# Turning q on VectorE and multiplying it in 32x64 tiles of the PE array

## The chip, the core and the metric

The kernel runs on one core of a Trainium2 chip. The metric is the device time of one execution in microseconds (us), the median of several runs. Five engines run side by side, each with its own stream of instructions, and wait for one another only through semaphores: TensorE (PE in the profile; its weight loads are a row of their own, PEld), VectorE (DVE), ScalarE (ACT), GpSimd (POOL) and SyncE (SP), which here starts most DMA transfers. TensorE writes its results to PSUM, which has eight banks of 512 fp32 values for each of 128 partitions. VectorE and ScalarE bring them from there to SBUF.

## What is computed

The program is an attention without softmax followed by a gated feed-forward block. All data are fp32.

```python
batch, n_heads, seq, head_dim = (8, 8, 576, 64)
n_tokens, d_model, d_ff = (4608, 512, 1536)

kv  = np.einsum('bhsd,bhse->bhde', k, v)              # 64 x 64 per head
out = np.einsum('bhsd,bhde->bhse', q, kv)
rms = np.sqrt(np.mean(out * out, axis=-1, keepdims=True) + 1e-06)
x   = (out / rms * g_norm)                            # then (B,H,S,D) -> (B*S, H*D)

gate = 1.0 / (1.0 + np.exp(-(x @ w_gate)))
val  = x @ w_val
return (gate * val @ w_out).astype(np.float32)
```

## The kernel before

The 4608 tokens are handled in nine chunks of 512 (`G`), so a chunk is a little less than one batch of 576. The first chunk and the attention of the first two batches are woven together by hand. From chunk 1 on, both dense layers use a Strassen-like scheme with 7 instead of 8 products (`first_layer_fast`, `second_layer_fast`); their lines are L578 and L664 of the profile. Attention works on pairs of heads: `n` is a pair, four of them (`NHP`) make a batch.

The attention of batch c+1 is put into the gaps of chunk c. It is cut into pieces, which wait in a queue `fill`. After each pair of products of the first dense layer, `slot()` takes one piece from the queue. A block of that layer has seven such slots, p1, p6, p2, p7, p5, p4 and p3, and a chunk has six blocks, so 42 slots.

```python
def slot():
    if fill:
        fill.popleft()()
...
for f in range(NF2):
    one, two = block(f), block(f + NF2)
    for i, (p, r) in enumerate(zip(one[0], two[0])):   # p1, p6, p2, p7, p5, p4, p3
        p()
        r()
        slot()
        ...                                            # sums of weights on GpSimd
    one[1]()                                           # VectorE: h = h * sg, 128x512
    two[1]()
    h_sums(c, f)                                       # VectorE: four sums of 128x256
```

These are the pieces of attention for one pair, as they were (marks of cuts are `...`):

```python
def q_mm():                         # L251: q turned by TensorE, six transposes of 96x128
    d["q"] = ps = at_ps("q")
    for j in range(NJ):
        c0 = NP * (j % JH)
        nc.tensor.transpose(ps[:, j // JH, c0:c0 + NP], pairs[n]["q"][:, j].rearrange("p e d -> p (e d)"),
                            ident[0:NP, 0:NP])

def q_out():                        # L256: copied to SBUF by ScalarE
    d["qT"] = sb.tile([P, 2, JH * NP], FP32, tag="qT", name="qT")
    nc.scalar.copy(out=d["qT"], in_=d["q"][:, :, 0:JH * NP])
    ...

def u_mm():                         # L271: q (k^T v) in tiles of 64 rows x 64 columns
    ps = at_ps("u")
    d["u"] = ps[:, :, 0:NU * HD]
    qT = d["qT"].rearrange("p i n -> p (i n)")
    for i in range(2 * NU):
        t0 = min(PH * i, S - PH)
        r = PH * (i % 2)
        for e in range(2):
            es = slice(HD * e, HD * e + HD)
            nc.tensor.matmul(d["u"][r:r + PH, e, HD * (i // 2):HD * (i // 2) + HD], qT[es, t0:t0 + PH], kv[es],
                             start=True, stop=True)
# then: u_square (ScalarE, 128x640), u_sum (VectorE), u_root (ScalarE), u_norm (VectorE),
# x_mm (L298: five transposes of 128x128 by TensorE), x_out (ScalarE, into xT, times g_norm)
```

The products k^T v of a batch are made at once, in 128x64 tiles (`kv_mm`, L332, and L338 for the rest of 64 tokens), and copied to SBUF by VectorE. The order in the queue was this:

```python
for n in range(NHP * b, NHP * b + NHP, 2):
    ...
    fill.extend([one[Q], one[Q_OUT], two_[Q], two_[Q_OUT]])
    if n == NHP * b:
        fill.extend([idle] * (0 if early else 3) + [kv_mm, kv_out])
    fill.extend([u_of_both, one[U_SQUARE], two_[U_SQUARE], one[U_SUM], two_[U_SUM], one[U_ROOT], one[U_NORM],
                 two_[U_ROOT], two_[U_NORM], one[X], one[X_OUT], two_[X], two_[X_OUT]])
```

In PSUM, attention has two tiles of two banks each, used in turn (`at_ps`), and the dense layers have four single banks (`mm_ps`).

Of the kernel before, what the change touches and what calls it, by code (L numbers as in the profile page):

```python
# [20 lines left out]
def kernel(  # L21
# [16 lines left out]
    P = 128  # L38
# [2 lines left out]
    NP = S // NJ  # L41
    JH = NJ // 2

    PH = P // 2
    NU = -(-S // P)
    UX = P * 3

    NK4 = S // P
    S4 = P * NK4
# [31 lines left out]
    def load_q(n):  # L81
        if n >= B * NHP:
            return
        b, h0 = n // NHP, 2 * (n % NHP)
        pool, bufs = (first, 4) if n < NE else (sb, 2)
        t = pool.tile([NP, NJ, 2, HD], FP32, tag="q", name="q", bufs=bufs)
        for e in range(2):
            nc.sync.dma_start(out=t[:, :, e, :], in_=q[b, h0 + e].rearrange("(p j) d -> p j d", j=NJ))  # L88
        pairs[n]["q"] = t

    kv_late = {}
# [118 lines left out]
    eps = const.tile([P, 1], FP32, name="eps")  # L210
    g_col = const.tile([P, 1], FP32, name="g_col")

    kvs = [const.tile([P, 2, HD], FP32, name=f"kv{i}") for i in range(2)]
    for e in range(2):
        nc.scalar.dma_start(out=g_col[HD * e:HD * e + HD], in_=g_norm.rearrange("(d o) -> d o", o=1))
    make_identity(nc, ident)
# [12 lines left out]
    def attention(n, at_ps):  # L229

        b, m = divmod(n, NHP)
        d = {}
        kv = kvs[n // 2 % 2][:, n % 2]

        def kv_mm():
            d["kv"] = ps = at_ps("kv")
            for j in range(NJ):
                js = slice(HD * j, HD * j + HD)
                for e in range(2):
                    nc.tensor.matmul(ps[HD * e:HD * e + HD, 0, 0:HD], pairs[n]["k"][:, e, js], pairs[n]["v"][:, e, js],  # L240
                                     start=(j == 0), stop=(j == NJ - 1))

        def kv_out():
            nc.vector.tensor_copy(out=kv, in_=d["kv"][:, 0, 0:HD])
            load_kv(n + 4)

        def q_mm():
# [4 lines that stand above are left out]
                                    ident[0:NP, 0:NP])  # L252

        def q_out():
            d["qT"] = sb.tile([P, 2, JH * NP], FP32, tag="qT", name="qT")
            nc.scalar.copy(out=d["qT"], in_=d["q"][:, :, 0:JH * NP])  # L256
            for i in (n + 4,) if n + 4 < NE else (n + 2,) if n + 2 >= NE else ():
                load_q(i)

        def u_mm():  # L260


            ps = at_ps("u")
            d["u"] = ps[:, :, 0:NU * HD]
            qT = d["qT"].rearrange("p i n -> p (i n)")
            for i in range(2 * NU):
                t0 = min(PH * i, S - PH)
                r = PH * (i % 2)
                for e in range(2):
                    es = slice(HD * e, HD * e + HD)  # L270
                    nc.tensor.matmul(d["u"][r:r + PH, e, HD * (i // 2):HD * (i // 2) + HD], qT[es, t0:t0 + PH], kv[es],  # L271
                                     start=True, stop=True)

        def u_square():
            d["sq"] = sb.tile([P, 2, NU * HD], FP32, tag="sq", name="sq")
            nc.scalar.activation(out=d["sq"], in_=d["u"], func=AF.Square)

        def u_sum():
            d["ms"] = sb.tile([P, 2, NU], FP32, tag="ms", name="ms")
            nc.vector.tensor_reduce(out=d["ms"].rearrange("p e i -> p (e i)"),  # L280
                                    in_=d["sq"].rearrange("p e (i d) -> p (e i) d", d=HD), axis=AX.X, op=ALU.add)

        def u_root():
            nc.scalar.activation(out=d["ms"], in_=d["ms"], func=AF.Sqrt, bias=eps, scale=1.0 / HD)

        def u_norm():

            nc.vector.reciprocal(d["ms"], d["ms"])
            d["xn"] = d["sq"].rearrange("p e c -> p (e c)")
            nc.vector.tensor_tensor(out=d["xn"].rearrange("p (i e d) -> p e i d", e=2, d=HD),  # L290
                                    in0=d["u"].rearrange("p e (i d) -> p e i d", d=HD),
                                    in1=d["ms"].unsqueeze(3).to_broadcast([P, 2, NU, HD]), op=ALU.mult)

        def x_mm():
            d["x"] = ps = at_ps("x")
            for i in range(NU):
                bank, c0 = divmod(P * i, UX)
                nc.tensor.transpose(ps[:, bank, c0:c0 + P], d["xn"][:, P * i:P * i + P], ident)  # L298

        def x_out():  # L300

            s0 = 0
            while s0 < S:
                c, o = divmod(S * b + s0, G)
                i, r = divmod(s0, UX)
                n_ = min(G - o, (UX if i == 0 else S - UX) - r)
                nc.scalar.activation(out=chunk(c)[:, m, o:o + n_], in_=d["x"][:, i, r:r + n_], func=AF.Copy, scale=g_col)
                s0 += n_

        return [kv_mm, kv_out, q_mm, q_out, u_mm, u_square, u_sum, u_root, u_norm, x_mm, x_out]  # L310


# [6 lines left out]
    def feed(b):  # L319
# [3 lines left out]

        def kv_mm():
            mains, rest = kv_late[b]
            tiles = [at_ps("kv") for _ in range(2)]
            d["kv"] = tiles
            for n in range(NHP):
                for j in range(NK4):
                    for e in range(2):  # L330
                        c = slice(NK4 * HD * e + HD * j, NK4 * HD * e + HD * j + HD)
                        nc.tensor.matmul(tiles[n // 2][HD * e:HD * e + HD, n % 2, 0:HD], mains[n, "k"][:, c],  # L332
                                         mains[n, "v"][:, c], start=(j == 0), stop=False)
            for i in range(NHP // 2):
                for r in range(2):
                    for e in range(2):
                        n, rs, c = NHP // 2 * r + i, slice(PH * r, PH * r + PH), HD * (2 * i + e)
                        nc.tensor.matmul(tiles[n // 2][HD * e:HD * e + HD, n % 2, 0:HD], rest[rs, c:c + HD],  # L338
                                         rest[rs, GH + c:GH + c + HD], start=False, stop=True)

        def kv_out():
            for kv, ps in zip(kvs, d["kv"]):
                nc.vector.tensor_copy(out=kv, in_=ps[:, :, 0:HD])

        def idle():
            pass

        for n in range(NHP * b, NHP * b + NHP, 2):
            one, two_ = (attention(n + i, at_ps) for i in range(2))

            def u_of_both(one=one, two_=two_):
                one[U]()
                two_[U]()

            fill.extend([one[Q], one[Q_OUT], two_[Q], two_[Q_OUT]])
            if n == NHP * b:
                fill.extend([idle] * (0 if early else 3) + [kv_mm, kv_out])
            fill.extend([u_of_both, one[U_SQUARE], two_[U_SQUARE], one[U_SUM], two_[U_SUM], one[U_ROOT], one[U_NORM],
                         two_[U_ROOT], two_[U_NORM], one[X], one[X_OUT], two_[X], two_[X_OUT]])

    def flush():
        while fill:
# [11 lines left out]
    def store(c, t, ot, cols=slice(0, DM), queues=(nc.sync,)):  # L374

        r0 = i = 0
        while r0 < P:
            b, s = divmod(G * c + P * t + r0, S)
            j, p = divmod(s, NP)
            n = min(P - r0, NP - p)  # L380
            dst = out[S * b:S * b + S, :].rearrange("(p j) d -> j p d", j=NJ)[j, p:p + n, cols]
            queues[i % len(queues)].dma_start(out=dst, in_=ot[r0:r0 + n, cols])
            r0 += n
            i += 1

    psum_at = ctx.enter_context(tc.tile_pool(name="psum_at", bufs=1, space=bass.MemoryType.PSUM))
    psum_ctx = tc.tile_pool(name="psum0", bufs=1, space=bass.MemoryType.PSUM)
    psum0 = psum_ctx.__enter__()  # L390

    def at0_ps():
        return psum_at.tile([P, 2, 512], FP32, tag="at", name="at")

    turns = count()

    def at_ps(kind):
        if next(turns) % 2 == 0:
            return at0_ps()
        return psum.tile([P, 2, 512], FP32, tag="at1", name="at1")  # L400

    def early(n):

# [8 lines left out]
                return t[:, :, JH * P:]  # L412
            return t
        return ps

    def mm_ps():
        return psum.tile([P, 512], FP32, tag="mm", name="mm", bufs=4)


    class Plain:  # L420
# [46 lines left out]
        b3.1.2 b3.0.3 b3.1.3 c4.4  # L467
    """
    blks, copies = {}, {}
    two0 = at0_ps()  # L470
    for token in order.split():
        name = token.rstrip("0123456789.")
        n = [int(i) for i in token[len(name):].split(".")]
# [1 line left out]
        if name == "b":  # L475
            if f not in blks:
# [2 lines left out]
                    psum = ctx.enter_context(tc.tile_pool(name="psum", bufs=1, space=bass.MemoryType.PSUM))  # L479
                    ps = (mm_ps(), mm_ps())  # L480
                else:
                    t = at0_ps() if f else two0
                    ps = (t[:, 0], t[:, 1])
                blks[f] = Plain(0, f, ps)
            blks[f].mm(n[1], n[2])
        elif name == "CG":
# [16 lines left out]
            load_unit(f)  # L503
        elif name == "warm":
            for _ in range(f):
                nc.tensor.matmul(two0[:, 0, 0:P], ident, ident, start=True, stop=True)
        else:
            a[f][steps[name]]()
            if token == f"Q{NE - 1}":
# [1 line left out]
                hp = ctx.enter_context(tc.tile_pool(name="hp", bufs=21))  # L511
    late.extend([blks[3].gate, blks[3].end])
    for f in range(4, NFT):
        plain(0, f, (mm_ps(), mm_ps()))
        if f == NFT - 2:
            load_late(2)

    two1 = [at_ps(None) for _ in range(2)]
    ps = [two1[t % 2][:, t // 2] for t in range(G // P)]

    def second(t, f):
        nc.tensor.matmul(ps[t], gv[0, f][:, P * t:P * t + P], w["wo", f], start=(f == 0), stop=(f == NFT - 1),  # L522
# [256 lines left out]
```

## Time and profile before

| | |
|---|---|
| time, median of 3 runs | 1097.55 us (1096.55 to 1098.04) |
| span of the profiled execution | 1095.0 us |
| TensorE clock granted | 1.00 |
| PE busy | 1088.9 us (99%) |
| DVE busy | 564.4 us (52%) |
| ACT busy | 315.7 us (29%) |
| POOL busy | 278.8 us (25%) |
| DMA moved | 57.73 MB, mean 53 GB/s |

The page of the profile gives busy times for the whole span, the chain of work that ended last, and the costliest groups of instructions. A group's line has the source line, the engine, the operation, the tile that it writes and the tiles that it reads, the shapes and the count, then the busy time in us and the mean of one in ns, and after a second bar the idle time of the engine just before, with what ended it. A matmul of fp32 leaves two records of its own and two of weight loads in the trace; a transpose leaves one of each. An answer by stretches of time gives, for each stretch, its length and what each engine was busy in it. An answer in order of time gives start and length in us, and merges instructions of one kind that follow one another.

### The profile page before, as it was taken

Reading aid. Unit: us, or ns where it says so; the run is one execution under the profiler, and the core shown is the slowest. Engines: PE = TensorE matmul, PEld = TensorE weight load, DVE = VectorE, ACT = ScalarE, POOL = GpSimd, SP = SyncE. Lnnn points to the kernel's source line nnn. Section 1 sums busy time; section 2 is a strip of 40 time slices with the busy share of each in tenths; the row PEclk is TensorE's granted clock in tenths of the full one; section 3 lists DMA queues with packets and bytes.
Section 4 is the critical chain, followed back from the end, with each engine's and each line's share of the span. In section 5 each row is a group of like instructions: output and inputs, shape, how many; then the busy total and the mean of one; then the engine's idle time right before and its main releaser. Section 6 shows DMA issues by size and latency. Waiting matters only on the chain.

```text
span 1095.0 us, 17063 instructions
## 1 busy us (share of the span) xinstructions
PE 1088.9 (99%) x6722; PEld 902.2 (82%) x6722; DVE 564.4 (52%) x1117; ACT 315.7 (29%) x611; POOL 278.8 (25%) x390
## 2 busy tenths in 40 slices
PE   9999999999999999999999999999999999999998
PEld 8544458888888888888888888888888888888888
DVE  4887845762366416561466236641656155615641
ACT  4754322421245114430254014511443011101110
POOL 0000024440244203330344024420333044404410
PEclk9999999999999999999999999999999999999999
DMA  9944711000400040101300040104000100010001
GB/s 246 265 156 154 240 39 23 10 14 20 128 1 22 15 124 11 23 1 50 98 22 1 20 128 1 23 13 119 18 1 1 30 10 1 1 38 2 1 1 39
DMA packets 81519, 57.73 MB, mean 53 GB/s; under 512 B 47392, under 2 KB 75424, under 8 KB 81440
## 3 DMA queue, kind: packets, MB, share of 16 engines
q1 hardware_dynamic: 81184, 56.61, 19.2%
q8 instruction: 54, 0.88, 0.3%
q14 instruction: 25, 0.20, 0.1%
q10 hardware_dynamic: 256, 0.03, 0.0%
HBM read 47.19 MB, written 9.44 MB: 52 GB/s over the span
## 4 chain that ended last, share of the span: by engine, by line
PE 97%; DMA 1%; SPq 1%; DVE 1%; issue 0%; ACT 0%; DVEq 0%
PE mm L578 53%; PE mm L664 26%; PE mm L427 6%; PE at L522 4%; PE at L427 2%; PE at L271 1%; PE at L298 1%; PE at L332 1%; PE at L251 1%; DMA v<-in_v_dram 1%; PE two L240 0%; PE two L271 0%; PE two L298 0%; PE two L251 0%; SPq L78 0%; SPq L88 0%
## 5 line engine op out<-in xcount | busy, mean ns | idle before, releaser
L565 POOL TENSOR_TENSOR tw<-gv 128x256 f32<-128x256 f32 x192 | 138.5, 732 | 765.9 <-PE mm L578 614.3
L578 PE MATMUL mm<-xT,tw 128*128 128x256 f32 x768 | 182.2, 380 | 0.2 <-DVE gv L592 0.2
L578 PE MATMUL mm<-sx,tw 128*128 128x256 f32 x768 | 182.3, 380 | 0.0
L578 PE MATMUL mm<-xT,gv 128*128 128x256 f32 x768 | 181.8, 380 | 0.0
L578 PEld LDWEIGHTS mm<-xT,gv 128*128 128x128 f32 x768 | 144.8, 190 | 19.7 <-issue 0.5
L578 PEld LDWEIGHTS mm<-xT,tw 128*128 128x128 f32 x768 | 144.1, 190 | 19.6 <-issue 0.6
L578 PEld LDWEIGHTS mm<-sx,tw 128*128 128x128 f32 x768 | 144.2, 190 | 19.0
L565 POOL TENSOR_TENSOR tw<-gv,tw 128x256 f32<-128x256 f32 x192 | 145.7, 780 | 0.0
L610 ACT ACTIVATE sg<-sg 128x256 f32<-128x256 f32 x96 | 40.0, 417 | 190.2 <-DVE sg L609 190.2
L600 DVE TENSOR_TENSOR gv<-mm,sg 128x256 f32<-128x256 f32 x96 | 40.8, 425 | 103.1 <-PE mm L578 103.1
L578 PE MATMUL mm<-sx,gv 128*128 128x256 f32 x384 | 91.3, 381 | 0.0
L664 PE MATMUL mm<-w,gv 128*128 128x256 f32 x384 | 88.5, 379 | 0.4 <-DVE gv L617 0.4
L664 PE MATMUL mm<-w,s 128*128 128x256 f32 (+1 forms) x408 | 88.3, 367 | 0.0
L664 PE MATMUL mm<-t2w,gv 128*128 128x256 f32 x384 | 88.1, 379 | 0.0
L586 ACT COPY sg<-mm 128x256 f32<-128x256 f32 x96 | 35.7, 372 | 165.9 <-PE mm L578 162.1
L617 DVE TENSOR_TENSOR gv<-gv,sg 128x512 f32<-128x512 f32 x96 | 82.6, 899 | 0.0
L664 PEld LDWEIGHTS mm<-w,s 128*128 128x128 f32 x408 | 74.1, 190 | 9.4
L664 PEld LDWEIGHTS mm<-w,gv 128*128 128x128 f32 x384 | 72.8, 190 | 10.6 <-DVE gv L617 0.8
L664 PEld LDWEIGHTS mm<-t2w,gv 128*128 128x128 f32 x384 | 72.9, 190 | 9.9
L578 PEld LDWEIGHTS mm<-sx,gv 128*128 128x128 f32 x384 | 72.5, 190 | 10.0
L596 ACT ACTIVATE sg<-mm 128x256 f32<-128x256 f32 x96 | 36.1, 383 | 106.3 <-PE mm L578 106.2
L614 DVE TENSOR_TENSOR gv<-mm,gv 128x256 f32<-128x256 f32 x96 | 40.7, 424 | 48.1 <-PE mm L578 48.1
(97 smaller groups left out, 1092.4 us busy)
## 6 DMA issues: line engine op xcount, KB each, us to landing
q<-in_q_dram SPq DMA_DIRECT2D x64, 144.0 KB, 3.1
st<-in_moe_w_gate_dram SPq DMA_DIRECT2D x12, 512.0 KB, 4.2
st<-in_moe_w_val_dram SPq DMA_DIRECT2D x12, 512.0 KB, 5.1
st<-in_moe_w_out_dram SPq DMA_DIRECT2D x12, 512.0 KB, 4.3
kv<-in_k_dram SPq DMA_DIRECT2D x24, 256.0 KB, 4.8
kv<-in_v_dram SPq DMA_DIRECT2D x24, 256.0 KB, 5.5
out_dram<-sg SPq DMA_DIRECT2D x23, 192.0 KB, 2.3
out_dram<-sg SPq DMA_DIRECT2D x24, 128.0 KB, 2.4
```

Of the source, the lines that this page charges most:

```text
L251: nc.tensor.transpose(ps[:, j // JH, c0:c0 + NP], pairs[n]["q"][:, j].rearrange("p e d -> p (e d)"), ident[0:NP, 0:NP])
L427: nc.tensor.matmul(self.ps[i], w[("wg", "wv")[i], self.f][:, m, :], xT[self.c][:, m, :], start=(m == 0), stop=(m == NMT - 1), skip_group_c ...
L522: nc.tensor.matmul(ps[t], gv[0, f][:, P * t:P * t + P], w["wo", f], start=(f == 0), stop=(f == NFT - 1), skip_group_check=True)
L565: nc.gpsimd.tensor_tensor(out=tw[f, i], in0=b[in0], in1=b[in1] if isinstance(in1, tuple) else tw[f, in1], op=ALU.subtract)
L578: nc.tensor.matmul(ps, wt[:, m, :], xs[:, m, :], start=(new and m == 0), stop=(m == NK - 1), skip_group_check=True)
L586: nc.scalar.copy(out=d["sg"][:, h2], in_=pa)
L596: nc.scalar.activation(out=d["sg"][:, h1], in_=d["pa"], func=AF.Sigmoid)
L600: tt(out=d["h"][:, h2], in0=d["pb"], in1=d["sg"][:, h2], op=ALU.add)
L610: nc.scalar.activation(out=d["sg"][:, h2], in_=d["sg"][:, h2], func=AF.Sigmoid)
L614: tt(out=d["h"][:, h1], in0=d["pc"], in1=d["h"][:, h1], op=ALU.add)
L617: tt(out=d["h"], in0=d["h"], in1=d["sg"], op=ALU.mult)
L664: nc.tensor.matmul(ps, hs(f), ws[:, f, :], start=(new and f == 0), stop=(f == NF2 - 1), skip_group_check=True)
```

## The change

Turning q leaves TensorE. VectorE transposes it in blocks of 32x32, which puts the 64 head dimensions of a head not on 64 partitions but on 32 partitions twice, for three row blocks of 32 tokens (`NQ = 3`) side by side. The contraction over 64 is therefore made in two steps of 32 (`NC = 2`), accumulated in PSUM, and it runs in tiles of 32 rows and 64 columns of the array: three row blocks by two column halves. Each row block needs k^T v on its own 32 partitions, so VectorE copies it there (`kv_copies`). The order of tokens within a batch changes with this, and the stores follow it.

Two pairs now go through the steps together, nine slots from their products to the transposes of x. That needs four PSUM banks in one piece for attention, in place of twice two; the dense layers still take four banks in turn, now from two pools of two. The tiles for turned q, for k^T v and for the squares are allocated once (`qTs`, `kvs`, `kvq`, `sqs`). The aim is to take work from TensorE.

```diff
@@ load_q
+        else:
+            t = sb.tile([NP, 2, NJ * HD], FP32, tag="q", name="q")
+            nc.sync.dma_start(out=t, in_=q[b, h0:h0 + 2].rearrange("h (p j) d -> p h (j d)", j=NJ))
@@ constants
-    kvs = [const.tile([P, 2, HD], FP32, name=f"kv{i}") for i in range(2)]
+    kvs = const.tile([P, NHP, HD], FP32, name="kvs")
+    kvq = const.tile([NP, NHP, 2 * NC, HD], FP32, name="kvq")
+    qTs = const.tile([P, 2, 2 * NJ * HD], FP32, name="qTs")
+    sqs = const.tile([P, 2 * NU * P], FP32, name="sqs")
@@ feed(b)
+        def kv_out():
+            nc.vector.tensor_copy(out=kvs, in_=d["kv"][:, :, 0:HD])
+
+        def kv_copies(i):
+            for r in range(NQ):
+                nc.vector.tensor_copy(out=kvq[QB * r:QB * r + QB, :, i], in_=kvs[QB * i:QB * i + QB])
+
+        def turn(n):
+            for e in range(2):
+                w_ = NJ * HD
+                nc.vector.transpose(qTs[0:NP, n % 2, w_ * e:w_ * e + w_],
+                                    pairs[n]["q"][:, e].rearrange("p (j i c) -> p i j c", i=NC, c=QB))
+            load_q(n + 2)
+
+        def two_pairs(n0):
...
+            def u_mm():
+                d["u"] = u = at_ps()[:, 0:NQ, 0:2 * QC]
+                for s in range(3):
+                    for e in range(2):
+                        for i in range(NC):
+                            for r in range(NQ):
+                                for half in range(2):
+                                    which, g = divmod(2 * s + half, 3)
+                                    c = NJ * HD * e + QC * i + PH * g
+                                    nc.tensor.matmul(u[PH * half:PH * half + PH, r, P * s + HD * e:P * s + HD * e + HD],
+                                                     qTs[QB * r:QB * r + QB, (n0 + which) % 2, c:c + PH],
+                                                     kvq[QB * r:QB * r + QB, (n0 + which) % NHP, NC * e + i],
+                                                     start=(i == 0), stop=(i == NC - 1))
...
+            def u_sum(i):            # half of the heads in a slot, and u_norm likewise
+                nc.vector.tensor_reduce(out=ms[:, :, units[i]], in_=by_head(sq)[:, :, units[i]], axis=AX.X, op=ALU.add)
...
+            def x_mm():
+                d["x"] = x = at_ps()
+                for r in range(NQ):
+                    for s in range(3):
+                        nc.tensor.transpose(x[:, r, P * s:P * s + P], sq[:, r, P * s:P * s + P], ident)
...
+            return [u_mm, u_square, lambda: u_sum(0), lambda: u_sum(1), u_root, lambda: u_norm(0), lambda: u_norm(1),
+                    idle, x_mm, lambda: x_out(0), lambda: x_out(1)]
@@ the queue
-        (the loop shown above)
+        n0 = NHP * b
+        fill.extend([lambda: turn(n0), lambda: turn(n0 + 1)] + [idle] * (0 if early else 5) + [kv_mm, kv_out])
+        fill.extend([lambda i=i: kv_copies(i) for i in range(2 * NC)])
+        fill.extend(two_pairs(n0))
+        fill.extend([lambda: turn(n0 + 2), lambda: turn(n0 + 3)])
+        fill.extend(two_pairs(n0 + 2))
@@ store: rows of batches from 2 on
+                r, c0 = divmod(s, QC)
+                n = min(P - r0, QC - c0)
+                queues[i % len(queues)].dma_start(
+                    out=rows.rearrange("(r p j) d -> r j p d", p=QB, j=NJ)[r, c0 // QB:(c0 + n) // QB],
+                    in_=ot[r0:r0 + n, cols])
@@ PSUM
+    def mm_ps():
+        if next(turns) % 4 < 2:
+            return psum.tile([P, 512], FP32, tag="mm", name="mm", bufs=2)
+        return mm0_ps()
+
+    def at_ps():
+        return psum.tile([P, 4, 512], FP32, tag="at", name="at")
@@ the end of chunk 0
-        plain(0, f, (mm_ps(), mm_ps()))
+        if f == NFT - 1:
+            last = at_ps()
+            plain(0, f, (last[:, 0], last[:, 1]))
+        else:
+            plain(0, f, (mm_ps(), mm_ps()))
...
-    two1 = [at_ps(None) for _ in range(2)]
-    ps = [two1[t % 2][:, t // 2] for t in range(G // P)]
+    ps = [mm_ps() for _ in range(G // P)]
```

## The prediction

> **What bounds the kernel now.** I read the engines' busy shares and the chain that ended last first, then busy time by stage, then the order in time of the weight loads around each piece of attention, and last the groups of VectorE. The page says that TensorE is the bound from end to end:
>
> ```profile
> PE 1088.9 (99%) x6722; PEld 902.2 (82%) x6722; DVE 564.4 (52%) x1117; ACT 315.7 (29%) x611; POOL 278.8 (25%) x390
> ...
> PE 97%; DMA 1%; SPq 1%; DVE 1%; issue 0%; ACT 0%; DVEq 0%
> ```
>
> A busy TensorE need not be a full one, so the reader should see what one chunk costs with and without attention. Below are two stretches (start:end, length, then busy time and instructions of PE, PEld, DVE, ACT, POOL). The first is a chunk of 512 tokens whose gaps hold the attention of one batch; the second is a chunk after the last batch, with the same two dense layers and nothing between.
>
> ```profile
> 636.40:755.10 118.70, 118.70 (x789) 104.18 (x789) 56.97 (x124) 35.83 (x72) 34.26 (x48) 1.00 0.15 40
> ...
> 873.80:982.60 108.80, 108.80 (x506) 95.78 (x505) 52.33 (x110) 15.55 (x40) 36.06 (x48) 1.00 0.04 10
> ```
>
> So one batch of attention adds 118.70 - 108.80 = 9.90 us, six times over (batches 2 to 7). The first two batches run in a hand-ordered start that the change leaves alone. What the change can win or lose is in these 6 x 9.9 = 59 us.
>
> Next the order in time of the weight loads. Without anything between them, one slot of dense work (8 loads) starts 1.73 us after the one before. In turn: a turn of q (L251), the products of two pairs (L271), five transposes of x (L298), the k^T v of a batch (L332, L338).
>
> ```profile
> 402.95 1.70 PEld L578 LDWEIGHTS mm<-xT,gv 128*128 128x128 f32 x8
> 404.68 0.69 PEld L251 LDWEIGHTS at<-ident,q 96*128 96x128 f32 x6
> 405.31 1.60 PEld L578 LDWEIGHTS mm<-xT,tw 128*128 128x128 f32 x8
> 406.93 1.70 PEld L578 LDWEIGHTS mm<-sx,tw 128*128 128x128 f32 x8
> ```
>
> ```profile
> 332.47 1.70 PEld L578 LDWEIGHTS mm<-xT,tw 128*128 128x128 f32 x8
> ...
> 334.50 1.26 PEld L271 LDWEIGHTS at<-kv,qT 64*64 64x64 f32 x80 [0.33 <-issue]
> ...
> 335.82 1.59 PEld L578 LDWEIGHTS mm<-sx,gv 128*128 128x128 f32 x8
> ...
> 337.44 1.70 PEld L578 LDWEIGHTS mm<-xT,gv 128*128 128x128 f32 x8
> ```
>
> ```profile
> 351.26 0.69 PEld L298 LDWEIGHTS at<-ident,sq 128*128 128x128 f32 x5
> 351.91 1.60 PEld L578 LDWEIGHTS mm<-sx,tw 128*128 128x128 f32 x8
> 353.53 1.70 PEld L578 LDWEIGHTS mm<-xT,gv 128*128 128x128 f32 x8
> ```
>
> ```profile
> 412.11 1.70 PEld L578 LDWEIGHTS mm<-xT,gv 128*128 128x128 f32 x8
> 414.14 1.95 PEld L332 LDWEIGHTS at<-kv 128*64 128x64 f32 x64 [0.33 <-issue]
> 416.16 0.32 PEld L338 LDWEIGHTS at<-kv 64*64 64x64 f32 x16
> 416.55 1.59 PEld L578 LDWEIGHTS mm<-sx,tw 128*128 128x128 f32 x8
> ```
>
> From the starts: a turn of q costs 405.31 - 404.68 = 0.63, and the slot behind it is 1.62 instead of 1.73, so 0.52 us net. Two pairs of products cost 0.30 of waiting before (334.50 - 332.47 = 2.03 instead of 1.73), 1.32 themselves, less 0.11: 1.51. Five transposes of x: 0.65 - 0.11 = 0.54. The k^T v: 0.30 + 2.41 - 0.11 = 2.60. Per batch 4 x 0.52 + 2 x 1.51 + 4 x 0.54 + 2.60 = 9.86, which is the 9.90 above: TensorE loses nothing to waits in these chunks, and what is taken from it counts in full.
>
> The tiles matter. In the products four tiles of 64x64 work side by side. Their 80 load records span 1.26 us less one load of 0.135, so 1.125 us for 20 rounds of four, 0.057 us a round. The k^T v has two tiles of 128x64: 64 records in 1.95 - 0.14 = 1.81 us are 32 rounds of two, also 0.057 us. A round of 64 columns costs the same whether two or four tiles share it, so the tile is the limit there and not the rate of issue.
>
> **What the Trainium skill says.** "TensorEngine Tiling (Array Packing)", section "Tiling Modes", gives eight tiles for 32x64, which load and multiply independently, and says that changing the mode drains the array; the constant round and the 0.30 us before L271 agree with both, for 64x64. Its section "Restrictions and Gotchas" wants different row tiles in different PSUM banks; the new code has row block r in bank r. "TensorE: Matmul & The Clock Gate", section "Wait — 56ns, not 53.3ns?", gives a floor of about 25 ns between starts of small matmuls. The trace has 80 records in 1.40 us, 17.5 ns each, below that; but these are 40 matmuls of the program, two records each, so 29 ns per matmul stay above it, and a floor per program matmul is not excluded. "VectorE: DVE Perf Modes", section "The three transpose paths", says that VectorE transposes within 32x32 blocks only and needs 311 ns for 128x128 of bf16; no run here shows it yet.
>
> **The change, part by part, per batch.**
> Turning q on TensorE goes: 4 x 0.52 = -2.08 us, with ScalarE's four copies of 0.64 us, off the path. VectorE now does it in 8 transposes of 96x384. Of the skill's 311 ns, 133 would be 128 elements at its 0.96 GHz, leaving 0.18; with 384 elements (0.40 us) that makes an estimate of 0.58 us each, 4.6 us in all.
> The products of two pairs become 72 program matmuls, 144 records, on six tiles (three row blocks by two column halves) instead of 80 records on four. If six tiles share a round as four did, that is 24 rounds of 0.057 = 1.37 us against 20 rounds = 1.14, so +0.23 for two pairs and +0.46 per batch. The entry and exit around it (1.51 - 1.14 = 0.37) stay.
> Turning x: nine transposes for two pairs in place of ten, at 0.54 / 5 = 0.108: -0.11 for two pairs, -0.22 per batch. Two pieces in place of four save little, as 0.54 is already five full transposes.
> The k^T v stays at 2.60. Behind it come 12 new copies of 32x256 on VectorE, which spread it over the row blocks.
> Sum on TensorE: -2.08 + 0.46 - 0.22 = -1.84 us per batch, six times -11.0 us.
>
> What VectorE gives back as waits. Its groups (line, engine, shapes, count, busy us, mean ns, idle before):
>
> ```profile
> L617 DVE TENSOR_TENSOR gv<-gv,sg 128x512 f32<-128x512 f32 x96 | 82.6, 899 | 0.0
> ...
> L592 DVE TENSOR_TENSOR gv<-mm,sg 128x256 f32<-128x256 f32 x96 | 38.3, 420 | 45.9 <-PE mm L578 45.2
> ...
> L280 DVE TENSOR_REDUCE ms<-sq 128x10 f32<-128x640 f32 x32 | 25.5, 810 | 4.5 <-ACT sq L276 4.5
> ...
> L343 DVE COPY kv<-at 128x128 f32<-128x128 f32 x12 | 2.9, 281 | 0.0
> ```
>
> A copy of 128 elements takes 281 ns, so I take 0.3 to 0.4 us for a new one of 256 from SBUF, about 4 us a batch. Reductions and products shrink a little (640 to 576 elements). VectorE rises from 57 to some 65 us of 117, no bound on average. But a slot holds 1.73 us, two adds out of PSUM take 0.84 of it, and a slot with three copies (1.0 us) or two transposes (1.16) overfills it. The copies fill four slots in a row and the second pair of turns two, and both end one slot before the products that need them. Following the slots by hand, with adds at 0.42, the copies end about as the slot between them is over, and the turns 0 to 0.4 us after the products could start. I take 0.2 us per batch, 1.2 in all. Chunk 1 is worse: the sums of the second layer's weights are woven in there, and this puts turns and copies around the long stretch of VectorE at a block's end (two products of up to 1 us and four sums of 0.42). I take 1 us once. Total -11.0 + 2.2 = -8.8: 1097.55 - 8.8 = 1088.75, rounded to 1089.
>
> **Rivals.**
> (a) Six tiles do not share a round. If 25 to 29 ns per program matmul is a floor of issue, 72 of them take 1.8 to 2.1 us and not 1.37: +0.9 to +1.4 per batch, leaving -0.9 to -0.4, a time of 1094 to 1097. Against it speaks the equal round with two and four tiles; for it, that nothing in this trace issued faster than 29 ns per matmul. One chance in four.
> (b) VectorE becomes the local bound. If a transpose of 4-byte data takes twice the estimate (1.1 us), the turns stack to 2.2 us a slot, and the products of the second half wait about 2 us per batch: +10 us more, 1098 to 1101. Nothing in the profile shows such a transpose, so I keep one in ten.
> (c) Buffers. Attention now has one tile of four banks instead of two of two, so a product waits for the previous copies into xT. At least two slots (3.5 us) of turning lie between, and those copies are below 1.5 us, so no wait. One DMA per pair of q with 1536-byte runs replaces two with 256-byte runs, and stores are cut at 192 rows and not at 96; the DMA is at a 15% share in these chunks, so both are hidden.
>
> **Range and chances.** Without waits it is 1086.5; a little extra at the start and end makes 1084.5 the low end. Rival (a) at half strength with some waits gives 1095.5 as the high end. A gain over 2% would need 22 us of 59, twice what the parts give: 0.02. A loss over 2% would need both rivals and more: 0.03. Within 2%: 0.95.
>
> **What would show it.** In the profile after: a chunk with attention should be 117.1 us (118.7 - 1.84 + 0.2) and the empty one still 108.8; the products' 144 load records should span about 1.5 us (2.2 with rival a); the transposes about 0.58 us each; and waits of TensorE for VectorE before the products should sum below 3 us. It is wrong if chunks stay at 118 or more, either because the products' records lie 13 ns or more apart, or because idle time before them is put down to a transpose or a copy.

## The result

The changed kernel takes 1116.1 us (median, 1112.51 to 1116.76) against 1097.15 before: 1.0165 times as long, 95% interval 1.0142 to 1.0188. It is slower, by 19 us, and far outside the predicted range. The page after, with the lines that answer to those of before:

```profile
PE 1091.4 (98%) x7334; PEld 902.0 (81%) x7334; DVE 617.2 (55%) x1219; ACT 267.3 (24%) x545; POOL 285.3 (26%) x390
...
HBM read 47.78 MB, written 9.44 MB: 51 GB/s over the span
...
PE 94%; DVE 4%; issue 1%; DMA 1%; SPq 0%; ACT 0%; POOL 0%; DVEq 0%; POOLq 0%
```

TensorE is still the bound, but it is now idle for 23.0 us (1114.4 - 1091.4) where it was idle for 6.1, and VectorE carries 4% of the chain where it carried 1%. One more line matters: the kernel reads 0.59 MB more from HBM than before, though the change adds no data. Before, it was:

```profile
HBM read 47.19 MB, written 9.44 MB: 52 GB/s over the span
```

By stretches, after: a chunk with attention, another one, the chunk without, the end with the last chunk, and the start. The columns are those of the prediction; the first of the last three is the granted clock, the second the DMA share, the third GB/s.

```profile
291.20:411.80 120.60, 119.67 (x892) 104.55 (x891) 66.17 (x141) 27.83 (x64) 35.34 (x48) 0.99 0.13 38
411.80:530.80 119.00, 118.08 (x892) 103.44 (x891) 66.19 (x141) 27.82 (x64) 35.35 (x48) 1.00 0.14 40
...
890.10:998.90 108.80, 108.80 (x506) 95.78 (x505) 52.32 (x110) 15.56 (x40) 36.04 (x48) 1.00 0.03 10
998.90:1114.40 115.50, 109.00 (x529) 96.40 (x527) 49.85 (x109) 15.55 (x40) 30.03 (x40) 0.99 0.05 14
0.00:171.40 171.40, 161.19 (x963) 86.94 (x964) 115.64 (x145) 72.35 (x104) 8.01 (x14) 0.97 0.61 176
```

Before, the same view has:

```profile
982.60:1095.00 112.40, 109.39 (x531) 96.75 (x529) 49.96 (x109) 15.55 (x40) 30.04 (x40) 1.00 0.05 14
0.00:160.70 160.70, 158.21 (x963) 84.95 (x964) 114.85 (x143) 72.51 (x104) 8.00 (x14) 1.00 0.67 184
```

The loss has three places. In the table, a boundary is the start of the first dense matmul of a chunk.

| stretch | before | after | difference |
|---|---|---|---|
| start, to chunk 1 | 160.6 | 171.3 | +10.7 |
| chunks 1 to 6, with attention | 713.5 | 718.7 | +5.2 |
| chunk 7, without | 108.8 | 108.8 | 0 |
| chunk 8 and the end | 112.1 | 115.6 | +3.5 |

### The profile page after: what moved, and what is told of

It is laid out like the page before. It is cut to its first block, busy times and chain, and to the rows that moved or that the text cites. A ratio compares the mean times of both kernels' runs of the same rounds, so it can differ in the third digit from the quotient of the medians.

```text
span 1114.4 us, 18252 instructions
## 1 busy us (share of the span) xinstructions
PE 1091.4 (98%) x7334; PEld 902.0 (81%) x7334; DVE 617.2 (55%) x1219; ACT 267.3 (24%) x545; POOL 285.3 (26%) x390
## 4 chain that ended last, share of the span: by engine, by line
PE 94%; DVE 4%; issue 1%; DMA 1%; SPq 0%; ACT 0%; POOL 0%; DVEq 0%; POOLq 0%
PE mm L669 49%; PE mm L755 26%; PE mm L516 7%; PE mm L613 4%; DVE kvq L358 2%; PE at L388 2%; PE at L344 1%; PE at L413 1%; PE mm L594 1%; PE at L516 1%; DMA q<-in_q_dram 1%; PE two L255 1%; PE two L284 0%; PE two L311 0%; PE two L266 0%
## 5 line engine op out<-in xcount | busy, mean ns | idle before, releaser
L669 PE MATMUL mm<-xT,gv 128*128 128x256 f32 x768 | 184.8, 384 | 0.0
L656 POOL TENSOR_TENSOR tw<-gv,tw 128x256 f32<-128x256 f32 x192 | 151.7, 811 | 0.2
L708 DVE TENSOR_TENSOR gv<-gv,sg 128x512 f32<-128x512 f32 x96 | 88.1, 956 | 0.0
L516 PE MATMUL mm<-xT,gv 128*128 128x512 f32 x176 | 79.5, 606 | 0.0
```

The lines of the kernel that those rows point to most:

```text
L516: nc.tensor.matmul(self.ps[i], w[("wg", "wv")[i], self.f][:, m, :], xT[self.c][:, m, :], start=(m == 0), stop=(m == NMT - 1), skip_group_c ...
L656: nc.gpsimd.tensor_tensor(out=tw[f, i], in0=b[in0], in1=b[in1] if isinstance(in1, tuple) else tw[f, in1], op=ALU.subtract)
L669: nc.tensor.matmul(ps, wt[:, m, :], xs[:, m, :], start=(new and m == 0), stop=(m == NK - 1), skip_group_check=True)
L708: tt(out=d["h"], in0=d["h"], in1=d["sg"], op=ALU.mult)
```

## The start: a load made twice

TensorE's longest waits after, from the view of waits, and its longest one in order of time:

```profile
PE two L266 <- DMA q<-in_q_dram: 8.2, 1, 8.2
PE at L388 <- DVE kvq L358: 4.6, 10, 0.5
```

```profile
45.44 1.19 PE L266 MATMUL two<-ident,q 96*128 96x96 f32 x6 [8.22 <-DMA q<-in_q_dram]
```

The transposes of q of pair 6 wait 8.2 us for a load. The reason is a part of the change that the diff above does not show. In `q_out`, the rule of which pair to load next was shortened:

```diff
-            for i in (n + 4,) if n + 4 < NE else (n + 2,) if n + 2 >= NE else ():
-                load_q(i)
+            load_q(n + 4 if n + 4 < NE else n + 2)
```

`NE` is 8. For n = 4 and 5 the old rule loads nothing, as pairs 6 and 7 were loaded by n = 2 and 3. The new rule loads them again, into the next buffers of the rotation, and the transposes take the later copy. Two pairs of 2 x 144 KB are 0.59 MB, the excess on the page. The second load of pair 6 is issued late:

```profile
37.99 2.12 SPq L95 DMA_DIRECT2D q<-in_q_dram  x2
```

In the kernel before, a load of q issued near this time took 8 us to land (35.54 to 43.47), and here the transposes, for which TensorE is free from about 37.2 on, begin at 45.44. Such a wait also costs afterwards:

```profile
37.00:45.00 8.00, 0.23 (x8) 0.09 (x4) 1.32 (x2) 0.51 (x2) 0.00 (x0) 0.78 1.16 281
45.00:50.00 5.00, 4.56 (x14) 3.04 (x15) 2.37 (x5) 1.14 (x3) 0.00 (x0) 0.50 1.10 267
```

The granted clock falls to half during the wait, and TensorE's next 5 us of work run at 0.50.

**e1: the one line undone.**

```diff
-            load_q(n + 4 if n + 4 < NE else n + 2)
+            for i in (n + 4,) if n + 4 < NE else (n + 2,) if n + 2 >= NE else ():
+                load_q(i)
```

> The changed kernel with one line undone: the loads of q for pairs 6 and 7 are issued once, not a second time after pairs 4 and 5. Theory A (the second load of pair 6 is what TensorE waits for in the start): HBM read falls from 47.78 to 47.19 MB, chunk 1 begins near 160.7 us instead of 171.4, and the time is about 1116.1 - 10.7 = 1105 us. Rival A2 (the start is slower through the new single tiles or the PSUM banks): chunk 1 still begins after 168 us and the time stays above 1113. In both the six chunks with attention stay at 119 to 120.6 us.

Measured: 1104.34 us, 1.0067 times before (1.0050 to 1.0084). HBM read is 47.19 MB and the wait for q is gone. The chunks were as long as in the changed kernel, 718.8 us for the six. Chunk 1 of the profiled run began at 163.3, not at 160.7, as TensorE waited 2.3 us for a load of v; that run took 1108.31, the other three 1103.5 to 1104.8. The later kernels with the same line began chunk 1 at 159.2 to 161.0, save one (e6: 163.8, again 2.7 us of waiting for v). Why v is late in some runs was not tried.

**e8: the kernel before, with the new rule alone.**

```diff
-            for i in (n + 4,) if n + 4 < NE else (n + 2,) if n + 2 >= NE else ():
-                load_q(i)
+            load_q(n + 4 if n + 4 < NE else n + 2)
```

> The kernel before, with the one line of loads as the change has it: q of pairs 6 and 7 is loaded twice. Theory A (the second load alone costs the start): HBM read rises from 47.19 to 47.78 MB, TensorE waits for the q of pair 6, chunk 1 starts 8 to 11 us later than 160.6, time 1105 to 1108. Rival A3 (it needs the new tiles or banks of the change to hurt): time 1097 to 1099.

Measured: 1110.58 us, 1.0132 times before (1.0115 to 1.0149). Its page and its waits:

```profile
HBM read 47.78 MB, written 9.44 MB: 52 GB/s over the span
```

```profile
PE two L251 <- DMA q<-in_q_dram: 12.2, 2, 11.7
```

Chunk 1 begins at 173.5 instead of 160.6, and every chunk after it is as long as before (713.5 us for the six). The second load alone costs 13 us there; it needs nothing else of the change. Theory A stands, A2 and A3 fall.

## The chunks: copies that end too late

With the start mended, a chunk still takes 119 to 121 us. In order of time, the first products of a batch in the changed kernel, at the end of the copies:

```profile
310.26 0.87 DVE L358 COPY kvq<-kvs 32x256 f32<-32x256 f32 x3
...
313.31 1.32 DVE L358 COPY kvq<-kvs 32x256 f32<-32x256 f32 x3
313.76 1.59 POOL L656 TENSOR_TENSOR tw<-gv 128x256 f32<-128x256 f32 x2 [8.56 <-PE mm L669]
...
315.45 2.21 DVE L358 COPY kvq<-kvs 32x256 f32<-32x256 f32 x3
...
317.93 0.68 PE L388 MATMUL at<-kvq,qTs 32*64 32x64 f32 x36
...
318.48 1.66 DVE L358 COPY kvq<-kvs 32x256 f32<-32x256 f32 x3
319.13 0.33 PE L388 MATMUL at<-kvq,qTs 32*64 32x64 f32 x4 [0.52 <-DVE kvq L358]
319.87 1.69 PE L388 MATMUL at<-kvq,qTs 32*64 32x64 f32 x104 [0.41 <-DVE kvq L358]
```

Three copies take 0.87 us while GpSimd rests, and 1.32, 2.21 and 1.66 once its sums of weights run from 313.76 on. The products begin at 317.93, do the 36 records whose data are there, and stop twice; the block ends 3.55 us after its start (the next loads are at 321.48) instead of 1.73. Of the 1.82 us more, 0.93 us are the two waits for copies; the rest passes between records for which the profile names no wait. The 1.82 us are the whole distance between a chunk of 119.0 us and the 117.2 us without such waits (e5 below). In two of the six chunks a second cost follows:

```profile
322.00:325.00 3.00, 3.00 (x9) 2.36 (x8) 1.64 (x5) 0.37 (x1) 0.00 (x0) 0.54 0.00 0
```

For 3 us after the pauses the granted clock is 0.54, so TensorE does half its work there. Chunks in which that happens take 120.6 us, the others about 119. Which chunks are hit differs between kernels. In the traces kept, no chunk without such pauses has it; why only some chunks with them do stays open. The lengths of the six chunks, each from its first dense matmul to that of the next chunk:

| kernel | six chunks, us | each |
|---|---|---|
| before | 713.5 | 119.9, 118.7, 118.7, 118.7, 118.7, 118.7 |
| changed | 718.7 | 119.8, 120.6, 119.0, 120.6, 119.3, 119.4 |
| e1 | 718.8 | 119.8, 120.6, 119.0, 119.0, 119.4, 121.0 |
| e2, copies on ScalarE | 706.1 | 118.7, 117.3, 117.6, 117.3, 117.9, 117.3 |
| e3, copies from PSUM | 719.6 | 120.6, 118.2, 118.9, 120.1, 123.5, 118.2 |
| e4, few GpSimd sums | 705.3 | 118.9, 117.2, 117.2, 117.2, 117.6, 117.2 |
| e5, a slot earlier | 705.8 | 119.1, 117.2, 117.4, 117.3, 117.7, 117.2 |
| e6, ScalarE and slack | 704.7 | 118.3, 117.2, 117.6, 117.2, 117.2, 117.2 |
| e7, two slots | 710.4 | 119.1, 118.2, 118.2, 118.3, 118.5, 118.2 |

All kernels from e2 to e7 contain the mended line of e1.

**e2: the copies on ScalarE.**

```diff
-                nc.vector.tensor_copy(out=kvq[QB * r:QB * r + QB, :, i], in_=kvs[QB * i:QB * i + QB])
+                nc.scalar.copy(out=kvq[QB * r:QB * r + QB, :, i], in_=kvs[QB * i:QB * i + QB])
```

> As e1, and the 12 copies of k^T v to the row blocks go from VectorE to ScalarE. Theory B (the copies on VectorE end too late for the first products of a batch, and TensorE waits for them and is throttled after some of these waits): chunks with attention fall to about 117.2 us, no wait of TensorE for the copies, no stretch of half clock, time about 1105 - 15.5 = 1090 us. Rival B2 (the chunks are longer because the 32x64 products are slow to issue): chunks stay at 119 us or more, time 1103 to 1106.

Measured: 1091.84 us, 0.9962 times before (0.9947 to 0.9977): faster than before. Chunks 2 to 6 take 117.3 to 117.9, with no wait of TensorE's matmuls for a copy; five of its weight loads, 0.3 us each, are put down to one, and that is the length of the pause that every such block begins with. Theory B stands. B2 falls for the bulk of the loss.

**e5: the same copies on VectorE, one slot earlier.**

```diff
-        fill.extend([lambda: turn(n0), lambda: turn(n0 + 1)] + [idle] * (0 if early else 5) + [kv_mm, kv_out])
+        fill.extend([lambda: turn(n0), lambda: turn(n0 + 1)] + [idle] * (0 if early else 4) + [kv_mm, kv_out])
         fill.extend([lambda i=i: kv_copies(i) for i in range(2 * NC)])
+        fill.append(idle)
         fill.extend(two_pairs(n0))
```

> As e1, with the k^T v of a batch, its eviction and its copies all one slot earlier, and an empty slot between the copies and the products (in chunk 1 only the empty slot). Copies stay on VectorE, from SBUF to SBUF. Theory B (the copies miss the products by up to 1.9 us): one slot of 1.73 us more takes almost the whole wait away, the half clock goes with it, chunks 117.2 to 117.6, time about 1090 to 1092. Rival B5 (VectorE's backlog moves with the copies and is paid elsewhere, as waits of the dense products): chunks stay above 118.5, time 1100 or more.

Measured: 1092.29 us, 0.9956 times before (0.9941 to 0.9971). The copies are as slow beside GpSimd as they were, and no product waits:

```profile
300.69 1.33 DVE L359 COPY kvq<-kvs 32x256 f32<-32x256 f32 x3
302.04 0.75 DVE L698 TENSOR_TENSOR gv<-mm,gv 128x256 f32<-128x256 f32 x2
302.83 2.20 DVE L359 COPY kvq<-kvs 32x256 f32<-32x256 f32 x3
```

The last three copies of this batch took 2.20 us beside GpSimd, and the products follow at 305.30, after they end at 305.03. VectorE's load is the same 66 us per chunk as in the changed kernel, so the average load was never the matter; one slot was. B5 falls: the dense products waited 1.1 us in the whole kernel.

**e3 and e4: what makes a copy slow.** In e3 the copies read k^T v from its PSUM tile and not from SBUF:

```diff
-                nc.vector.tensor_copy(out=kvq[QB * r:QB * r + QB, :, i], in_=kvs[QB * i:QB * i + QB])
+                nc.vector.tensor_copy(out=kvq[QB * r:QB * r + QB, :, i],
+                                      in_=d["kv"][QB * i:QB * i + QB, :, 0:HD])
```

> As e1, with the 12 copies still on VectorE but read from PSUM instead of SBUF. Theory B3 (a copy from SBUF to SBUF is slowed by GpSimd's sums, which read SBUF at the same time: 0.29 us alone and 0.44 to 0.74 beside them): copies take an even 0.39 to 0.42 us whatever GpSimd does, 5 us a batch instead of 5.6, they end about 0.5 us earlier, chunks 117.3 to 118.5, time 1091 to 1098. Rival B4 (VectorE's slots are simply overfull, GpSimd does not matter): the copies vary as before with a mean near 0.47 and chunks stay at 119 or more, time 1103 to 1106.

e4 leaves out most of GpSimd's sums of weights: block 0 makes its sums once, and all blocks of all chunks use them.

```diff
     def w_sum(f, i):
+        if f in (0, NF2) and (f, i) in tw or f not in (0, NF2):
+            tw[f, i] = tw[0 if f < NF2 else NF2, i]
+            return
```

> As e1, but GpSimd makes the sums of weights for the first block only and all blocks use those; the other sums are left out, so the output differs. Copies stay on VectorE from SBUF to SBUF. Theory B3: each copy takes 0.29 us, TensorE waits for none, chunks about 117.2 us or less, time near 1090. Rival B4: copies keep a mean near 0.47 us and TensorE still waits for them, chunks 119, time near 1104.

The copies' lines in e1, e3 and e4 give the shortest, median and longest in ns:

```profile
L359 DVE COPY kvq<-kvs x72: 274/289/737, 178.6 to 789.9; 32x256 f32<-32x256 f32 x72
```

```profile
L359 DVE COPY kvq<-at x72: 402/419/430, 174.4 to 787.8; 32x256 f32<-32x256 f32 x72
```

```profile
L359 DVE COPY kvq<-kvs x72: 271/284/289, 174.9 to 774.1; 32x256 f32<-32x256 f32 x72
```

From SBUF beside GpSimd up to 737 ns; from PSUM at most 430 beside the same GpSimd; from SBUF with nearly all of GpSimd's sums left out at most 289. So it is GpSimd, and only for the copy that reads SBUF. The Trainium skill, "VectorE: DVE Perf Modes", section "Two Vector instructions with no wait between them", says that VectorE's second SBUF read interface is shared with GpSimd and that an operation of one input uses it in a two-port mode. These three lines fit that; that the copy runs in such a mode is inferred, as no run shows the mode itself. The median of 289 ns hides the slow copies: about half of the 72 run while GpSimd rests.

In time, e4 did as theory B3 expected (1091.03 us in one run). e3 did not: 1106.77 us, 1.0091 times before (1.0062 to 1.0120), in runs from 1102.8 to 1110.3. The waits of TensorE in e3 show a part of why:

```profile
PE at L390 <- DVE kvq L359: 5.2, 6, 1.0
PE mm L671 <- issue: 2.0, 2, 1.6
PE at L390 <- issue: 1.7, 1, 1.7
```

The products write the same four banks that the copies now read. They can't begin before the last copy has read its bank, whereas in the changed kernel the first 36 records went ahead. A block so starts 1.0 us late but then runs through in most chunks, and where nothing else happens a chunk takes 118.2 us (chunks 2 and 6), as theory B3 expected. Chunks 4 and 5 also have pauses of 1.6 and 1.7 us for which the profile shows no release, and in chunk 5 the granted clock is 0.50 from 667.6 to 674.4. What makes these pauses stays open. So the theory of a slow copy is shown by the durations and by e4, not by the time of e3.

**e6: copies on ScalarE and slack.** As e2, with the empty slot of e5, and one more after the second pair of turns:

```diff
         fill.extend([lambda: turn(n0 + 2), lambda: turn(n0 + 3)])
+        fill.append(idle)
         fill.extend(two_pairs(n0 + 2))
```

> As e2 (copies on ScalarE), with the slot of slack of e5 and one more empty slot between the second pair of turns and their products. If the remaining waits (1.7 us for copies, 1.1 us for turns, most of them in chunk 1) are all that is left above the parts, chunk 1 falls from 118.7 to about 117.5 and the others to 117.2, time 1089.5 to 1091. If the slack costs elsewhere, the time is at or above the 1091.8 of e2.

Measured: 1091.32 us, 0.9955 times before (0.9939 to 0.9971). Chunk 1 falls to 118.3, not to 117.5; the wait for the turns (1.0 us, once) is gone. Against e2 and e5 this is no difference that the runs can tell.

## The products themselves

A block of products that waits for nothing, and nine transposes of x, in the changed kernel:

```profile
344.67 1.70 PEld L669 LDWEIGHTS mm<-xT,tw 128*128 128x128 f32 x8
346.70 1.66 PEld L388 LDWEIGHTS at<-kvq,qTs 32*64 32x64 f32 x144 [0.33 <-issue]
348.43 1.59 PEld L669 LDWEIGHTS mm<-sx,gv 128*128 128x128 f32 x8
...
362.14 1.12 PEld L413 LDWEIGHTS at<-ident,sqs 128*128 128x128 f32 x9
363.23 1.60 PEld L669 LDWEIGHTS mm<-xT,gv 128*128 128x128 f32 x8
```

Two pairs cost 0.30 + 1.73 - 0.11 = 1.92 us (1.51 before, 1.74 predicted), the transposes 1.09 - 0.11 = 0.98 (0.97 predicted). The records span 1.66 - 0.13 = 1.53 us, against 1.37 for 24 plain rounds. The single starts in the trace show the pace of the rounds, 12 records in 117 ns, so six in 58 ns as with two and four tiles, and in between a few pauses of about 20 to 45 ns.

**e7: the 72 products in two slots.**

```diff
-            def u_mm():
-                d["u"] = u = at_ps()[:, 0:NQ, 0:2 * QC]
+            def u_mm(part):
+                if part == 0:
+                    d["u"] = at_ps()[:, 0:NQ, 0:2 * QC]
+                u = d["u"]
                 for s in range(3):
                     for e in range(2):
+                        if (2 * s + e) // 3 != part:
+                            continue
...
-            return [u_mm, u_square,
+            return [lambda: u_mm(0), lambda: u_mm(1), u_square,
```

> As e2, with the 72 products of two pairs in two slots, 36 in each. In the changed kernel the first 36 records of a block of 144 start in rounds of six per 0.058 us, and the other 108 at 0.0114 us each. Theory C (TensorE's instructions run ahead while it is busy with long products; a block starts from a full queue and falls to the rate of issue when that is empty): each half starts fast again, 0.35 us for its first 36 records, and then slows, so a half spans about 0.75 us and a block's two halves together 1.5 us less the second entry, while each entry costs 0.3 to 0.4 us more: chunks 0.5 to 0.7 us longer than in e2. Rival C2 (the slow part belongs to those products, by their banks or data): the first half slows after 36 records and the second is slow from its first round.

```profile
333.91 0.92 PEld L393 LDWEIGHTS at<-kvq,qTs 32*64 32x64 f32 x72 [0.33 <-issue]
...
336.82 0.91 PEld L393 LDWEIGHTS at<-kvq,qTs 32*64 32x64 f32 x72 [0.33 <-issue]
```

Both halves take the same, 0.92 and 0.91 us, each a little above its 12 rounds (0.68 + 0.13), and a chunk is on average 0.7 us longer than in e2 for the second entries (1096.93 us in one run). The single starts of the two halves follow the same pattern from the first record to the last, so the slow places do not belong to certain products, and C2 falls. The sizes are near those of theory C (a half spans 0.79 us, expected 0.75), but its mechanism is not shown: after the first 36 records the pace is still 12 in 117 ns, and what is lost lies in the pauses. What makes the pauses stays open. They cost 0.18 us per block, 2.2 us in all.

## The end: transfers on four DMA engines

The last matmul of the changed kernel ends at about 1107.9, 6.5 us before the end; before it was 3.0 us. In these microseconds nothing but the last stores runs:

```profile
1110.00:1111.00 1.00, 0.00 (x0) 0.00 (x0) 0.00 (x0) 0.00 (x0) 0.00 (x0) 1.00 0.26 97
1111.00:1112.00 1.00, 0.00 (x0) 0.00 (x0) 0.00 (x0) 0.00 (x0) 0.00 (x0) 1.00 0.28 88
```

A share of about a quarter is what 4 of 16 DMA engines give when they never rest. The share alone does not prove it, for it was as low at the very end before, but only after a microsecond of 0.70:

```profile
1091.00:1092.00 1.00, 0.99 (x9) 0.80 (x8) 0.00 (x0) 0.00 (x0) 0.00 (x0) 1.00 0.70 207
1092.00:1093.00 1.00, 0.00 (x0) 0.00 (x0) 0.29 (x1) 0.00 (x0) 0.00 (x0) 1.00 0.21 55
1093.00:1094.00 1.00, 0.00 (x0) 0.00 (x0) 0.00 (x0) 0.00 (x0) 0.00 (x0) 1.00 0.27 66
```

A store of 128 rows is now a pattern of 4 j by 32 rows; before, up to 96 rows of one j lay outermost. The Trainium skill, "DMA: Bandwidth & Descriptors", section "Why a DMA increments its semaphore by 16 and not by 1", says that the slowest dimension that isn't 1 sets how many of the 16 engines share a transfer, the largest number up to 16 that divides it on both sides. For 4 x 32 that is four.

**e9 and e10: the last chunk's stores cut smaller**, on top of e6; e10 has `2 * QB`.

```diff
                 n = min(P - r0, QC - c0)
+                if c == NG - 1:
+                    n = min(n, QB)
```

> As e6, with the stores of the last chunk cut to 32 rows each, so that a transfer has one row block of one j and not four. In the changed kernel 6.5 us pass between TensorE's last matmul and the end, against 3.0 before, with DMA at a share of 0.17 to 0.28 in these microseconds. Theory D (a transfer whose rows come as j x 32 is spread over few of the 16 DMA engines, about one for each j, and so ends late): the end comes about 3 us after the last matmul again, the DMA share rises above 0.4 for about 1 us, and the time is about 1091.3 - 3.4 = 1088 us. Rival D2 (the stores are late for the scattered rows in DRAM or for the number of transfers): the end stays 6 us or more behind, time 1091 or more.

> As e9, but cut to 64 rows, two j in a transfer. Theory D: a transfer is spread over about two engines, so the last ones take as long as with four j or longer, DMA share 0.25 or less at the end, which comes 5 us or more after the last matmul. If the size of a transfer alone counts, it lies between e6 and e9.

Measured: e9 takes 1088.33 us, 0.9924 times before (0.9910 to 0.9937), and ends 3.4 us after its last matmul (1082.96 to 1086.33). e10 took 1096.37 in one run, and ends 10.4 us after it (1084.1 to 1094.5). Their last stretches, e9 first:

```profile
1082.30:1083.30 1.00, 0.66 (x6) 0.46 (x5) 0.29 (x1) 0.00 (x0) 0.00 (x0) 1.00 0.61 152
1083.30:1084.30 1.00, 0.00 (x0) 0.00 (x0) 0.00 (x0) 0.00 (x0) 0.00 (x0) 1.00 0.30 69
```

```profile
1089.50:1090.50 1.00, 0.00 (x0) 0.00 (x0) 0.00 (x0) 0.00 (x0) 0.00 (x0) 0.50 0.13 46
1090.50:1091.50 1.00, 0.00 (x0) 0.00 (x0) 0.00 (x0) 0.00 (x0) 0.00 (x0) 0.50 0.14 43
```

Two j in a transfer hold the share at 0.13 to 0.14, as two engines of sixteen would; four j gave 0.26; and in e9 it rose to 0.61 for a microsecond, as expected. The single DMA packets of the traces say the same: after the last matmul, four packets of data are under way at most moments in the changed kernel and never more than six, two in e10 and never more than four, while at the end of the kernel before and of e9 there are up to 17. The end comes 3.5 us later than before with four j and 7.4 us later with two, about double, as with half the engines. Transfers of half the size were slower and of a quarter faster, so neither size nor number is it, and the scattered rows are the same in all three: D2 falls and theory D stands. In the chunks between, such slow stores are hidden: the chunk without attention takes 108.8 us in every kernel.

e9 is the fastest kernel of the study, 8.3 us below before.

## The prediction, step by step

- **"A hand-ordered start that the change leaves alone"**: this is the step that failed most, +10.7 us. The change does touch it, as the rule of loads in `q_out` is shared by the start, and the second load, seen in HBM bytes, stops TensorE for 8.2 us and halves its clock after. e1 and e8 show it from both sides.
- **"I take 0.2 us per batch"** of waiting for copies and turns (and 1 us for chunk 1): mis-sized. The six chunks took 718.7 us, where the prediction's sums come to 704.7 (713.5 - 8.8); with one slot of slack, e5 took 705.8. So 12.9 us of waits, of slow blocks around them and of half clock went with that one slot, where 2.2 us had been allowed in all. The 1 us for the turns in chunk 1 came as estimated (1.0 us, once). The slots were followed with copies of 0.3 to 0.4 us each. Alone they take 0.29, but beside GpSimd up to 0.74; I saw the same stretch in L617 (two of them in 1.28 or in 2.08 us) and did not apply it.
- **The stores "both hidden"** in rival (c): wrong for the last ones, +3.5 us. The prediction looked at the length of the runs and at the share, not at the outermost dimension of the pattern.
- **The sum on TensorE**, -1.84 us per batch: right in kind. Measured without waits, a chunk is 117.2 us, -1.5. The turns of q and of x came as worked out; the term that was off is the products, +0.41 for two pairs and not +0.23.
- **The transposes on VectorE**, 0.58 us: measured 0.548. Rival (b), slow transposes, did not happen. Its other half did: VectorE became the local bound, by the copies.
- **Rival (a)**, tiles that do not share a round: no. 72 products in 1.53 us are 21 ns each, below the 25 to 29 ns that the rival took for a floor. Six tiles share a round, with pauses.
- **The range**: its low end supposed that the start and the end could only shift a little. e9, the changed kernel with four further edits, lies at 1088.33, near the predicted 1089, because it takes away the causes that the prediction did not have. That it comes so near is in part luck: the products cost 2.2 us more than predicted, and of the 2.2 us allowed for waits little is left.

## What to carry to other kernels

An engine at 99% gains what you take off it only if every producer still comes in time: give the consumer a slot of slack before you trust a sum of durations, since a copy may take two and a half times as long beside another engine. When a diff shortens a condition, run it through for every index, and compare the bytes read on the two pages. Where rows are reordered, look at the outermost dimension of each transfer: four there went with a share of four DMA engines, which cost nothing in the middle of this kernel and 3.5 us at its end.

## What was not expected of the hardware

- A VectorE copy of 32x256 fp32 from SBUF took 0.27 to 0.29 us alone and up to 0.74 beside GpSimd; from PSUM 0.40 to 0.43 either way.
- After two waits of TensorE of 0.4 to 0.5 us within one block of small products, the granted clock fell to 0.54 over the next 3 us in some chunks and not in others; such chunks are 1.6 us longer. It may also be why the changed kernel's runs spread over 4 us, as the fastest has the highest mean clock (0.994, the others 0.990 to 0.992), but only one was profiled.
- Six tiles of 32x64 keep the round of 58 ns that two and four tiles have, apart from the pauses.
- Stores with four, two and one j outermost ended 6.5, 10.4 and 3.4 us after the last matmul.
